# Start addresses of loaded tiles, the order of the last loads, and a permuted read of o, in a decode kernel that is bound by its loads

## Chip, cores and metric

One core of a Trainium2 chip; the other cores idle. The metric is the device time of one execution in microseconds (us), median of several. The kernel before takes 533.47 us (533.46 to 534.03, three runs).

## The reference, cut to what matters

```python
x  = A_x                                   # 4 x 1 x 640, bf16
xn = layernorm(x)
# A: attention of one new token, 32 heads of 192, over the last 2048 of 8192 cached keys
q  = xn @ wq                               # 640 -> 32*192
p  = softmax(q . k_cache[:, :, -2048:] * 192**-0.5)
oA = (p @ v_cache[:, :, -2048:]) @ wo      # 6144 -> 640
# B: gated feed-forward, 640 -> 1536 -> 640
oB = (silu(xn @ w1) * (xn @ w3)) @ w2
return x + oA + oB
```

K and V of the window are 32 heads x 4 sequences x 2048 x 192 x 2 B, twice: 201 MB of the 223 MB that are loaded. Each byte is used once, and the loads set the pace: their queue keeps the DMA engines busy for 98.6% of the span before.

## The kernel before, as far as the change touches it

```python
    const = ctx.enter_context(tc.tile_pool(name="const", bufs=1))      # x, masks, qbc, ...
    fpool = ctx.enter_context(tc.tile_pool(name="ffn", bufs=1))        # w1, w3, w2 in turn
    kpool = ctx.enter_context(tc.tile_pool(name="kt", bufs=KBUFS))     # 2 tiles of 24,576 B a partition
    vpool = ctx.enter_context(tc.tile_pool(name="vt", bufs=VBUFS))     # 3
    ppool = ctx.enter_context(tc.tile_pool(name="pr", bufs=PBUFS))
    wopool = ctx.enter_context(tc.tile_pool(name="wo", bufs=2))
    # ... cut
    def load_v(h):                         # load_k likewise
        vt = vpool.tile([P, NJ, Dh], BF16, tag="vt")
        nc.sync.dma_start(out=vt[:].rearrange("q j d -> q (j d)"),
                          in_=v_win[:, h].rearrange("b (p j) d -> p b (j d)", p=PB))
    # ... cut
    def ge_sum(h):                         # head sum: adds the four strips of o of one head
        for par in range(2):
            nc.tensor.matmul(po[sl, 0:Dh], lhsT=sel_w[:, par]..., rhs=o_sb[:, par * Dh:(par + 1) * Dh], ...)
    def ge_turn(hg):                       # divides by the softmax sums and turns o
        nc.vector.tensor_scalar_mul(out=og[:].rearrange("p i r -> p r i"),
                                    in0=po[:, 0:Dh].rearrange("p (r i) -> p r i", i=RPP), scalar1=...)
        nc.vector.transpose(out=oT..., in_=og...)
    # ... cut: the schedule is a list of slots; one slot is a quarter of a head
    # tail: K31 | V29, V30, V31, w2 first part, wo 7, w2 second, w2 third   (wo 6 ahead of K31)
```

A load of K or V goes to 128 partitions, one contiguous row of 24,576 B each. A head's path: multiply K by q on the vector engine (`mult`, tile pr), add on the tensor engine (`adder`, tile ps), softmax, weighted sum of V (`pv`, tile o_ps), head sum (tile po), and for every four heads a projection by wo into acc.

## Time and profile before

| | before |
|---|---|
| time, median | 533.47 us |
| span of the profiled run | 530.5 us |
| loaded | 222.97 MB |
| mean of a 24,576 B packet (slow ones over 1.2 of the median left out) | 916.4 ns |
| last load lands | 526.85 us |
| cast of the result starts | 527.44 us |

How to read it: a "packet" is one row of one load. The records of the kernel before hold 128 such packets for each load but those of x, and for each 16 packets of 4 B (the completion writes of the recorded texts, 9 ns each), and a load has 16 semaphore steps, one for each DMA engine. The records don't name the engine; but from one load's finish to the next an engine takes 7.315 us, eight rows of 914 ns, so I count 8 of the 128 rows of each load to an engine, 640 rows of data in the whole run. "Lands" is the last of the 16 steps, that is, the slowest engine: multiplies that wait for K start 0.02 us after it in the kernel before, and 1.85 to 4.78 us after the first step. Packet durations and semaphore steps are in the trace's records; no line of the page holds them.

### The profile page before, as it was taken

The numbers are of one execution on the slowest core, as the hardware profiler recorded it, in microseconds if no ns is written. First come the engines' busy times: TensorE is split into PE (matmuls) and PEld (weight loads), VectorE is DVE, ScalarE is ACT, GpSimd is POOL, SyncE is SP. The second block draws the span as 40 slices with busy tenths as digits, with TensorE's granted clock in tenths as the row PEclk, the third lists the DMA queues.
The fourth block names the chain that finished last, engine by engine and source line by source line (L and its number), as shares of the span: only waits on it lengthen the run. The fifth ranks groups of instructions, "written<-read, shape, count | busy, mean of one in ns | idle before, by whom it ended". The sixth has DMA issues, their size and how long they took to land.

```text
span 530.5 us, 5427 instructions
## 1 busy us (share of the span) xinstructions
PE 342.7 (65%) x2306; PEld 144.5 (27%) x2307; DVE 350.2 (66%) x435; ACT 45.6 (9%) x143; POOL 1.1 (0%) x8
## 2 busy tenths in 40 slices
PE   2765766674757586667558776576565775566774
PEld 1322322232312232223223232232222232222332
DVE  3179775775557667578646876676667776667941
ACT  2111100000201000000000000000000000000010
POOL 0000000000000000000000000000000000000000
PEclk9889988899858878789988897798997899889988
DMA  8999999999999999999999999999999999999995
GB/s 356 445 417 422 417 435 434 426 434 422 431 434 421 433 423 433 430 426 433 426 423 437 424 428 429 428 432 424 428 429 432 427 432 426 432 427 406 428 427 220
DMA packets 11575, 223.31 MB, mean 421 GB/s; under 512 B 1296, under 2 KB 1312, under 8 KB 2592
## 3 DMA queue, kind: packets, MB, share of 16 engines
q1 hardware_dynamic: 11536, 222.97, 98.6%
q8 instruction: 18, 0.29, 0.2%
q14 instruction: 5, 0.04, 0.0%
q10 hardware_dynamic: 16, 0.01, 0.0%
HBM read 222.96 MB, written 0.01 MB: 420 GB/s over the span
## 4 chain that ended last, share of the span: by engine, by line
DMA 60%; DVE 23%; PE 15%; ACT 1%; issue 1%; SPq 0%
DMA kt<-in_A_k_cache_dram 50%; DVE pr L215 15%; PE ps L226 8%; DMA w<-in_B_w_dram 6%; DVE sc L234 4%; DMA wt<-in_A_wq_dram 3%; PE qps L175 2%; PE po L303 2%; DVE og L308 1%; DVE z L270 1%; PE o_ps L278 1%; ACT ex L262 1%; PE acc L196 1%; DVE oT L311 1%; ACT L262 0%
## 5 line engine op out<-in xcount | busy, mean ns | idle before, releaser
L226 PE MATMUL ps<-pr,idb 128*128 128x512 bf16 x768 | 212.5, 418 | 161.8 <-DVE pr L215 161.8
L215 DVE TENSOR_TENSOR pr<-kt,qbc 128x3072 bf16<-128x3072 bf16 x128 | 223.3, 1745 | 110.6 <-DMA kt<-in_A_k_cache_dram 110.6
L226 PEld LDWEIGHTS <-idb 128*128 128x128 bf16 x768 | 76.2, 103 | 262.8 <-issue 206.4
L234 DVE TENSOR_REDUCE sc<-ps 128x16 f32<-128x512 f32 x128 | 87.0, 679 | 1.9 <-PE ps L226 1.9
L278 PE MATMUL o_ps<-vt,z 128*8 128x384 bf16 x1024 | 55.0, 353 | 5.5 <-DMA vt<-in_A_v_cache_dram 5.5
L303 PE MATMUL po<-o_sb,sel_w 128*32 128x192 f32 x128 | 35.0, 409 | 0.5 <-ACT o_sb L285 0.5
L278 PEld LDWEIGHTS <-z 128*8 128x8 bf16 x1024 | 25.1, 90 | 31.8 <-issue 20.4
L285 ACT COPY o_sb<-o_ps 128x384 f32<-128x384 f32 x32 | 15.3, 479 | 193.6 <-PE o_ps L278 193.6
L259 ACT COPY negm<-mt 128x1 f32<-128x1 f32 x32 | 5.1, 159 | 258.0 <-PE mt L256 258.0
L270 DVE TENSOR_TENSOR z<-ex,mask_b 128x256 bf16<-128x256 bf16 x32 | 13.4, 417 | 18.2 <-ACT ex L262 18.1
L175 PE MATMUL qps<-wt,xnT 128*128 128x512 bf16 x59 | 16.6, 443 | 5.1 <-DMA wt<-in_A_wq_dram 5.1
L303 PEld LDWEIGHTS po<-o_sb,sel_w 128*32 128x32 f32 x128 | 13.8, 130 | 20.9 <-issue 14.5
L181 DVE CAST qbc<-qps 128x512 bf16<-128x512 f32 x6 | 3.8, 685 | 18.5 <-PE qps L175 18.5
L308 DVE TENSOR_SCALAR og<-po,rt 128x192 bf16<-128x192 f32 x8 | 8.4, 1055 | 8.0 <-PE po L303 8.0
L248 DVE TENSOR_REDUCE gmax<-mt 1x4 f32<-1x128 f32 x32 | 8.8, 276 | 6.9 <-PE mt L243 6.8
L256 PEld LDWEIGHTS mt<-ones_ff,gneg 1*128 1x128 f32 x64 | 9.4, 182 | 13.4 <-issue 8.1
L256 PE MATMUL mt<-ones_ff,gneg 1*128 1x1 f32 x64 | 12.1, 256 | 0.0
L243 PE MATMUL mt<-idf,lmax 128*1 128x128 f32 x32 | 11.2, 351 | 1.1 <-DVE lmax L238 1.1
L196 PE MATMUL acc<-wo_t,oT 128*4 128x320 bf16 x96 | 10.3, 318 | 1.6 <-DVE oT L311 1.6
L262 ACT ACTIVATE ex<-sc,negm 128x64 bf16<-128x64 f32 x32 | 11.1, 348 | 1.0
L175 PEld LDWEIGHTS <-xnT 128*128 128x128 bf16 x60 | 6.6, 110 | 14.7 <-issue 9.1
L290 PEld LDWEIGHTS po<-rsum,tot_w 128*32 128x32 f32 x64 | 4.7, 112 | 14.7 <-issue 13.1
(52 smaller groups left out, 70.2 us busy)
## 6 DMA issues: line engine op xcount, KB each, us to landing
kt<-in_A_k_cache_dram SPq DMA_DIRECT2D x32, 3072.0 KB, 20.2
vt<-in_A_v_cache_dram SPq DMA_DIRECT2D x32, 3072.0 KB, 27.4
wo_t<-in_A_wo_dram SPq DMA_DIRECT2D x8, 960.0 KB, 21.0
wt<-in_A_wq_dram SPq DMA_DIRECT2D x2, 3072.0 KB, 9.8
w<-in_B_w_dram SPq DMA_DIRECT2D x2, 1920.0 KB, 25.0
wt<-in_A_wq_dram SPq DMA_DIRECT2D x1, 1536.0 KB
w<-in_B_w_dram SPq DMA_DIRECT2D x1, 1280.0 KB, 34.3
w<-in_B_w_dram SPq DMA_DIRECT2D x2, 320.0 KB, 36.4
```

The costliest lines, as they stand in the source:

```text
L175: nc.tensor.matmul(qp[:], lhsT=xnT[:, kc].rearrange("p a b -> p (a b)"), rhs=wq_rows[kc][:, (c0 + i) * QC:(c0 + i + 1) * QC], start=(kc == ...
L196: nc.tensor.matmul(acc[i * CT:i * CT + B, :], lhsT=lhsT, rhs=rhs[:, i * N0:(i + 1) * N0], start=first, stop=last)
L215: nc.vector.tensor_tensor(out=pr[:], in0=kts[h][:, g * JQ:(g + 1) * JQ, :], in1=qbc[:, h * Dh:(h + 1) * Dh].unsqueeze(1).to_broadcast([P, ...
L226: nc.tensor.matmul(ps[:], lhsT=idb[:], rhs=pr[:, :, kk * DD:(kk + 1) * DD], start=(kk == 0), stop=(kk == NK - 1))
L234: nc.vector.tensor_reduce(out=scs[h][:, g * JQ:(g + 1) * JQ], in_=pss.pop(u)[:], axis=AX.X, op=ALU.add)
L256: nc.tensor.matmul(mt[:, P:P + 1], lhsT=gneg[:].rearrange("o p b -> o (p b)"), rhs=ones_ff[0:1, 0:1], start=True, stop=True)
L262: nc.scalar.activation(out=ex[:], in_=scs.pop(h)[:], func=ACTF.Exp, bias=negm[:, 0:1], scale=SCALE, accum_out=rsum[:])
L270: nc.vector.tensor_tensor(out=z[:], in0=ex[:].unsqueeze(2).to_broadcast([P, NJ, B]), in1=mask_b[:].unsqueeze(1).to_broadcast([P, NJ, B]), ...
L278: nc.tensor.matmul(o_ps[c * CT:c * CT + 2 * B, :], lhsT=z[:, 2 * jj:2 * jj + 2, :], rhs=vt[:, 2 * jj:2 * jj + 2, :], start=(jj < 4), stop= ...
L285: nc.scalar.copy(out=o_sb[:], in_=o_ps[:])
L303: nc.tensor.matmul(po[sl, 0:Dh], lhsT=sel_w[:, par].rearrange("p a b -> p (a b)"), rhs=o_sb[:, par * Dh:(par + 1) * Dh], start=(par == 0), ...
L308: nc.vector.tensor_scalar_mul(out=og[:].rearrange("p i r -> p r i"), in0=po[:, 0:Dh].rearrange("p (r i) -> p r i", i=RPP), scalar1=rts.pop ...
```

## The change

The intent is threefold. The pools with loaded tiles go ahead of the constants, so that every loaded tile starts at a multiple of 256 B (before: 32 B past one). The last loads go in another order: V29 ahead of K31, V31 in halves, wo 6 behind the first part of w2. And o is permuted while the tensor engine reads it for the head sum, so that the vector engine writes it in order.

```diff
-    const = ctx.enter_context(tc.tile_pool(name="const", bufs=1))
+    head = ctx.enter_context(tc.tile_pool(name="head", bufs=1))
     fpool = ...; kpool = ...; vpool = ...
+    wopool = ctx.enter_context(tc.tile_pool(name="wo", bufs=2))
+    const = ctx.enter_context(tc.tile_pool(name="const", bufs=1))
     ppool = ...
-    wopool = ctx.enter_context(tc.tile_pool(name="wo", bufs=2))
 # ... cut: load_v(h, parts=1) loads in `parts` pieces along the row
-    tot_w = const.tile([P, NREP, B], FP32, name="tot_w")
+    tot_w = head.tile([P, NREP, B], FP32, name="tot_w")        # 128 B: brings the next pool to 256
 # ge_sum
-                             rhs=o_sb[:, par * Dh:(par + 1) * Dh], ...
+                             rhs=o_sb[:, par * Dh:(par + 1) * Dh].rearrange("p (r i) -> p i r", i=RPP), ...
 # ge_turn
-        nc.vector.tensor_scalar_mul(out=og[:].rearrange("p i r -> p r i"),
-                                    in0=po[:, 0:Dh].rearrange("p (r i) -> p r i", i=RPP), ...
+        nc.vector.tensor_scalar_mul(out=og[:].rearrange("p i r -> p (i r)"), in0=po[:, 0:Dh], ...
 # schedule
-        if h < H - 3:
+        if h < H - 2:
             add(u0 + 2, 0, load_v, h)
-    for h in range(H - 3, H):
-        add(NU - 6, 0, load_v, h)
+    for h in range(H - 2, H):
+        add(NU - 6, 0, load_v, h, 1 + (h == H - 1))
     add(NU - 6, 0, w2_load, 0)
+    add(NU - 6, 0, wo_load, NG - 2)
     add(NU - 6, 0, wo_load, NG - 1)
 # ... cut: pv of head 31 in halves, projection of wo 6 moved behind w2's first part
```

More of the change, by code (lines that the diff above doesn't have):

```diff
@@ L93, in load_k, with load_v @@
         kts[h] = kt
-    def load_v(h):
+    def load_v(h, parts=1):
         vt = vpool.tile([P, NJ, Dh], BF16, tag="vt")
-        nc.sync.dma_start(out=vt[:].rearrange("q j d -> q (j d)"),
-                          in_=v_win[:, h].rearrange("b (p j) d -> p b (j d)", p=PB))
+        src = v_win[:, h].rearrange("b (p j) d -> p b j d", p=PB)
+        n = NJ // parts
+        for j in range(0, NJ, n):
+            nc.sync.dma_start(out=vt[:, j:j + n, :].rearrange("q j d -> q (j d)"),
+                              in_=src[:, :, j:j + n, :].rearrange("p b j d -> p b (j d)"))
         vts[h] = vt
@@ L303, in ge_sum @@
             nc.tensor.matmul(po[sl, 0:Dh], lhsT=sel_w[:, par].rearrange("p a b -> p (a b)"),
-                             rhs=o_sb[:, par * Dh:(par + 1) * Dh], start=(par == 0), stop=(par == 1))
+                             rhs=o_sb[:, par * Dh:(par + 1) * Dh].rearrange("p (r i) -> p i r", i=RPP), start=(par == 0), stop=(par == 1))
     def ge_turn(hg):
         og = small.tile([P, RPP, CT], BF16, tag="og", bufs=1, name="og")
-        nc.vector.tensor_scalar_mul(out=og[:].rearrange("p i r -> p r i"),
-                                    in0=po[:, 0:Dh].rearrange("p (r i) -> p r i", i=RPP), scalar1=rts.pop(hg)[:, 0:1])
+        nc.vector.tensor_scalar_mul(out=og[:].rearrange("p i r -> p (i r)"), in0=po[:, 0:Dh],
+                                    scalar1=rts.pop(hg)[:, 0:1])
         oT = small.tile([P, RPP, CT], BF16, tag="oT", bufs=2, name="oT")
@@ L387 @@
         v, m = ends.get(h, (u0 + L, u0 + L + 1))
-        add(v, 7, pv, h)
+        if h < H - 1:
+            add(v, 7, pv, h)
+        else:
+            add(v - 1, 7, pv, h, 0, NJ // 2)
+            add(v, 7, pv, h, NJ // 2, NJ)
         add(m, 7, ge_sum, h)
@@ L407 @@
     add(17, 6, x_add, 1)
-    add((H - 3) * GQ + 1, 0, wo_load, NG - 2)
-    add(NU - 4, 6, ge_proj, NG - 2, 0, RPP // 2)
-    add(NU - 3, 6, ge_proj, NG - 2, RPP // 2, RPP)
-    for h in range(H - 3, H):
-        add(NU - 6, 0, load_v, h)
+    for h in range(H - 2, H):
+        add(NU - 6, 0, load_v, h, 1 + (h == H - 1))
     add(NU - 6, 0, w2_load, 0)
+    add(NU - 6, 0, wo_load, NG - 2)
     add(NU - 6, 0, wo_load, NG - 1)
@@ L418 @@
     add(NU - 6, 0, w2_load, 2)
-    add(e - 2, 8, ffn_out, 0)
+    add(e - 1, 8, ffn_out, 0)
+    add(e - 1, 8, ge_proj, NG - 2, 0, RPP)
     add(e, 6, ge_proj, NG - 1, 0, RPP)
```

## The prediction

Its windows are pieces of 256 B that start at multiples of 256 B: a row of 24,576 B touches 96 of them, and 97 where the tile starts 32 B past a multiple. That each costs the same 9.41 ns (913 ns in 97 parts) is my estimate from packet durations; no run had shown it.

> **What bounds the kernel now.** I read the page first: busy shares, the DMA row and the queues.
>
> ```profile
> span 530.5 us, 5427 instructions
> PE 342.7 (65%) x2306; PEld 144.5 (27%) x2307; DVE 350.2 (66%) x435; ACT 45.6 (9%) x143; POOL 1.1 (0%) x8
> DMA  8999999999999999999999999999999999999995
> q1 hardware_dynamic: 11536, 222.97, 98.6%
> ```
>
> No engine is over 66%; the queue of loads keeps the 16 DMA engines busy for 98.6% of the span. Next, the chain of work that ended last, half of it K loads:
>
> ```profile
> 83.94 1.77 DVE pr L215
> ...
> 113.18 1.76 DVE pr L215
> ...
> 444.28 1.76 DVE pr L215
> ...
> 473.53 1.77 DVE pr L215
> ```
>
> Each of these multiplies starts when its K lands. In both pairs four loads of 3072 KB pass, in 29.24 and 29.25 us: 7.31 us a load. A DMA engine carries 8 of the 128 rows of 24,576 B, so a row costs 914 ns. The trace's packet records agree: 8,448 packets of 24,576 B, one a row, median 915 ns.
>
> Third, do loads come late? The queue's waits, its issues, and the stretches of time:
>
> ```profile
> SPq L91 <- DVE pr L215: 323.9, 30, 13.0
> ...
> 41.02 0.54 SPq L91 DMA_DIRECT2D kt<-in_A_k_cache_dram  x1
> ...
> 485.09 0.53 SPq L91 DMA_DIRECT2D kt<-in_A_k_cache_dram  x1
> ```
>
> ```profile
> 42.00:44.00 2.00, 1.19 (x7) 0.43 (x6) 1.97 (x3) 0.00 (x0) 0.00 (x0) 1.00 0.87 307
> 60.00:480.00 420.00, 274.71 (x1866) 114.66 (x1865) 285.70 (x345) 31.59 (x108) 0.00 (x0) 0.88 1.00 429
> 485.00:487.00 2.00, 1.88 (x21) 0.79 (x24) 0.67 (x2) 0.00 (x0) 0.00 (x0) 1.00 0.90 324
> 525.00:527.00 2.00, 1.13 (x18) 0.80 (x20) 0.78 (x2) 0.00 (x0) 0.00 (x0) 1.00 0.17 64
> ```
>
> The last two columns are DMA share and GB/s. The issuing queue waits 324 us and it costs nothing: between 60 and 480 us the share is 1.00, because two more loads lie behind the one under way. The rings run dry twice, behind the issues at 41.02 and 485.09 us. At the end some engines finish early (share 0.17 in the last stretch). The semaphore records say how far apart the 16 engines are: the wo load before K31 finishes on its first engine at 485.71 and on its last at 490.48 us. From there to the last engine's finish of V30 at 512.42 us are 21.94 us, three loads of 7.31: the slowest engine never starved at 485 us. Only the quick ones did, and only the slowest sets the end. Its last piece of w2 lands at 526.85 us, and the timeline ends so:
>
> ```profile
> 525.87 0.98 PE L196 MATMUL acc<-wo_t,oT 128*4 128x320 bf16 x12 [1.57 <-DVE oT L311]
> 526.69 0.71 PE L196 MATMUL acc<-w,hT 128*4 128x320 bf16 x8
> 527.44 0.48 DVE L430 CAST res<-acc 36x320 bf16<-36x320 f32 x1 [1.62 <-PE acc L196]
> ```
>
> The result's cast starts 0.59 us after that landing; the last projection is ready at about the same time, so two paths end together.
>
> [...] In the built program of before every K, V, wq, wo and FFN tile starts 32 B past such a multiple[...]
>
> **The change, part by part.** (a) Alignment. The built program of after has all loaded tiles but the small x tiles at multiples of 256 B. My model, made from packet durations: each touched window of 256 B costs [...]9.41 ns, however few bytes are in it. It gives 97 x 9.41 = 913 ns for 24,576 B (trace 912 to 922), 31 x 9.41 = 292 for 7,680 B (trace 291 to 301, median 294), 49 x 9.41 = 461 for 12,288 B (trace 460), and one, 9.4, for the completion write of 4 B (trace 9). Aligned, each row sheds one. Rows: K and V 64 x 128 = 8,192, wq 384, wo 1,024, w1, w3 and w2 640: 10,240, or 640 an engine; 640 x 9.41 ns = 6.02 us. Not all of it reaches the end. The K issue at 41.02 us waits for multiplies behind the q projection, which follows only the wq loads. Those save 24 rows, 0.23 us; the next 24 rows (two K, one V) save another 0.23 us into an already dry ring. Left: 5.80 us. (b) V31 in halves: one more completion write an engine, 0.01 us lost. (c) V29 before K31, wo 6 at the end: the dry stretch at 485 us should go, but the slowest engine lost nothing there, so 0, though the sums of busy time will look better. (d) The tail: after V31 now come w2's first part, two wo and two small parts of w2: by the model 321 + 241 + 241 + 81 + 81 = 965 windows, 9.1 us, where before V31 landed 7.1 us ahead of the end. V31's second half needs its weighted sum (half of 2.73 us), copy 0.48, the head sum about 1.3, og, oT 0.38, projection 0.98: under 6 us, so it is now hidden. Alignment alone would have left this chain of some 7.6 us the later of the two, by about 0.3 us: the new order protects that and gains up to 0.1. (e) o permuted as the moving operand: eight og of 1.05 us become contiguous, about 0.3 us each (estimate from the qbc cast, 512 columns in 685 ns). 6 us of DVE, none on the path. The matmuls of the head sum (128 records, 35.0 us) read 4 B at a step of 24 B. If that doubles them PE gets 35 us more work and reaches 71% of the span: still no bound. Sum: 5.80 - 0.01 + 0.1, about 5.9 us; 533.47 - 5.9 = 527.6.
>
> **Rivals.** First, the 9 ns a packet are a fixed cost (turnaround) and not the extra window. For it: 4 B also take 9 ns, so an intercept of 9 ns fits all sizes. Against it: [...]the records have 9 and 29, which are one and three windows.[...] I give it one in eight. Second, the dry stretch at 485 us did cost the end, or the engines' lag comes out smaller: bytes missing in 485 to 490 us make about 0.75 us of all engines' time; the time would be 526.8. Third, the slow read of o becomes a wait: at the end, if the head sum took three times as long, V31's chain would pass the last w2 landing. The slack is some 3 us against 2.6 us more; unlikely, and then worth under 1 us: 528.5. Fourth, slow packets of about 1.4 us (23 between 60 and 480 us) make the slowest engine late; they may fall otherwise in the changed program, up to 1 us either way.
>
> **Range and chances.** The model explains the load rate to 0.1%, so most chance lies near 527.6, with the lag's 1 us either way and a tail for the first rival: 526.3 to 529.8 for 8 in 10. Faster by over 2% would be below 522.8 us[...]; 0.02. Slower by 2% needs a new bound: 0.01. Within 2%: 0.97.
>
> **What would show it.** Rows of 24,576 B at a median of about 905 ns in place of 915; four loads between K landings in 28.95 us (4 x 769 windows); GB/s of 433 to 434 in mid-kernel; no dry stretch near 480 us; the last w2 landing near 521 us, and the cast 0.5 to 0.6 us after it; og near 0.3 us; the head-sum matmuls dearer or not, with no change of the end. Wrong: rows still at 913 to 915 ns (first rival), or a cast that waits for the V31 chain.

## The result, and the profile after

The changed kernel takes 529.56 us (529.35 to 531.62, four runs) where the one before took 533.55 on the same occasion. The ratio is 0.9932, with a 95% interval of 0.9907 to 0.9957. Ratios here are the mean time of one kernel's fast runs over that of the other's of the same rounds, so not quite the ratio of the medians that I quote. A repeat on another chip gave 529.22 us and 0.9906 (0.9890 to 0.9923). So the gain is between 3.6 and 5.0 us; the forecast was 5.9. By the threshold of 2% the two are the same.

The page of the changed kernel, lines that answer to those of before:

```profile
span 527.6 us, 5428 instructions
PE 353.5 (67%) x2306; PEld 142.6 (27%) x2307; DVE 345.6 (65%) x435; ACT 45.6 (9%) x143; POOL 1.1 (0%) x8
DMA  8999999999999999999999999999999999999994
q1 hardware_dynamic: 11680, 222.97, 98.6%
```

The picture is the same: loads all the time, no engine near its limit. The chain of work that ended last:

```profile
411.38 1.76 DVE pr L219
...
440.47 1.77 DVE pr L219
...
469.56 1.76 DVE pr L219
```

Four loads now take 29.09 us in place of 29.25; I had forecast 28.95. Half of the step is there. The stretches of time (last two columns: DMA share and GB/s):

```profile
42.00:44.00 2.00, 1.19 (x6) 0.47 (x5) 1.97 (x3) 0.00 (x0) 0.00 (x0) 1.00 0.71 258
60.00:480.00 420.00, 283.87 (x1886) 113.91 (x1885) 287.68 (x352) 32.80 (x114) 0.00 (x0) 0.89 1.00 431
485.00:487.00 2.00, 1.06 (x3) 0.39 (x3) 1.97 (x4) 0.00 (x0) 0.00 (x0) 0.78 1.00 430
```

431 GB/s and not the forecast 433 to 434. The dry stretch at 485 us is gone, the one at 42 us is not. The packet records say what happened to a row (durations in ns, packets over 1.2 of the median left out):

```
packet of        24,576 B             7,680   10,240   12,288   15,360   2,560 B
before  mean     916.4                295.8   389.0    460.0    578.0    104.9
        most     915, 922, 912, 914   294     388      460      576      102
after   mean     912.2                291.0   385.0    460.0    573.0    102.0
        most     912 (99% 912 or 913) 291     385      460      573      102
```

Alignment took away the spread above the shortest duration and left the shortest where it was. Misaligned rows had been at 912 ns too: 303 of the 304 that start between 4 and 25 us in the kernel before are at 912 or 913 ns, the first rows of K among them. A load takes 7.275 us in place of 7.315, read from one finish of the first of the 16 engines to the next (81.89, 96.43, 110.99 us; before 82.06, 96.69, 111.32; two loads between each): 5.0 ns a row. (The row of 12,288 B is of wq, before the spread set in, and of V31's halves after.)

The end of the timeline, against 525.87, 526.69 and 527.44 us before:

```profile
523.05 0.98 PE L200 MATMUL acc<-wo_t,oT 128*4 128x320 bf16 x12 [0.40 <-DVE oT L315]
523.86 0.71 PE L200 MATMUL acc<-w,hT 128*4 128x320 bf16 x8
524.62 0.48 DVE L437 CAST res<-acc 36x320 bf16<-36x320 f32 x1 [1.62 <-PE acc L200]
```

The last load lands at 523.85 us, 3.00 us earlier; the cast starts 0.77 us after it (before 0.59). The projection still comes from oT and not from a landing: two paths still end together. And the groups of instructions for o (busy us and mean ns of one stand behind the first bar), on the page of before and then on the listing of after:

```profile
L303 PE MATMUL po<-o_sb,sel_w 128*32 128x192 f32 x128 | 35.0, 409 | 0.5 <-ACT o_sb L285 0.5
L308 DVE TENSOR_SCALAR og<-po,rt 128x192 bf16<-128x192 f32 x8 | 8.4, 1055 | 8.0 <-PE po L303 8.0
```

```profile
L307 PE MATMUL po<-o_sb,sel_w 128*32 128x192 f32 x128 | 49.1, 517 | 1.1 <-ACT o_sb L289 1.1
L312 DVE TENSOR_SCALAR og<-po,rt 128x192 bf16<-128x192 f32 x8 | 3.2, 404 | 3.7 <-PE po L307 3.6
```

og fell to 404 ns, the head sum's records rose from 409 to 517 ns mean; neither bounds anything.

### The profile page after: what moved, and what is told of

Its sections match the earlier page's. It is cut to its first block, busy times and chain, and to the rows that moved or that the text cites.

```text
span 527.6 us, 5428 instructions
## 1 busy us (share of the span) xinstructions
PE 353.5 (67%) x2306; PEld 142.6 (27%) x2307; DVE 345.6 (65%) x435; ACT 45.6 (9%) x143; POOL 1.1 (0%) x8
## 3 DMA queue, kind: packets, MB, share of 16 engines
q1 hardware_dynamic: 11680, 222.97, 98.6%
## 4 chain that ended last, share of the span: by engine, by line
DMA 57%; DVE 22%; PE 18%; ACT 2%; issue 1%; SPq 0%
DMA kt<-in_A_k_cache_dram 54%; DVE pr L219 15%; PE ps L230 9%; PE po L307 4%; DVE sc L238 3%; DMA wt<-in_A_wq_dram 3%; PE qps L179 2%; PE o_ps L282 2%; DVE z L274 1%; ACT ex L266 1%; PE mt L260 1%; DVE oT L315 1%; DVE og L312 0%; PE acc L200 0%; ACT L266 0%
## 5 line engine op out<-in xcount | busy, mean ns | idle before, releaser
L230 PE MATMUL ps<-pr,idb 128*128 128x512 bf16 x768 | 208.5, 412 | 152.3 <-DVE pr L219 152.3
L230 PEld LDWEIGHTS <-idb 128*128 128x128 bf16 x768 | 74.4, 102 | 258.7 <-issue 200.1
L282 PE MATMUL o_ps<-vt,z 128*8 128x384 bf16 x1024 | 60.6, 373 | 2.7 <-DMA vt<-in_A_v_cache_dram 2.7
L307 PE MATMUL po<-o_sb,sel_w 128*32 128x192 f32 x128 | 49.1, 517 | 1.1 <-ACT o_sb L289 1.1
L282 PEld LDWEIGHTS <-z 128*8 128x8 bf16 x1024 | 26.2, 94 | 32.8 <-issue 22.8
L200 PE MATMUL acc<-wo_t,oT 128*4 128x320 bf16 x96 | 9.2, 298 | 0.4 <-DVE oT L315 0.4
L242 DVE TENSOR_REDUCE lmax<-sc 128x1 f32<-128x64 f32 x32 | 7.0, 220 | 1.1
```

The lines of the kernel that those rows point to most:

```text
L200: nc.tensor.matmul(acc[i * CT:i * CT + B, :], lhsT=lhsT, rhs=rhs[:, i * N0:(i + 1) * N0], start=first, stop=last)
L230: nc.tensor.matmul(ps[:], lhsT=idb[:], rhs=pr[:, :, kk * DD:(kk + 1) * DD], start=(kk == 0), stop=(kk == NK - 1))
L282: nc.tensor.matmul(o_ps[c * CT:c * CT + 2 * B, :], lhsT=z[:, 2 * jj:2 * jj + 2, :], rhs=vt[:, 2 * jj:2 * jj + 2, :], start=(jj < 4), stop= ...
L307: nc.tensor.matmul(po[sl, 0:Dh], lhsT=sel_w[:, par].rearrange("p a b -> p (a b)"), rhs=o_sb[:, par * Dh:(par + 1) * Dh].rearrange("p (r i) ...
```

## The experiments

Theory A: alignment brings the gain, by taking the spread off the packets; about 8 ns a packet stay, as a fixed cost (7.8 ns by the aligned sizes, below). Rivals: the load order brings it; or the place of the constants. For the engines' lag, theory D: fetches of tensor instructions. "Last landing" and "lag" (first to last engine at that landing; the expectations call it the spread) are of the profiled run.

| run | time, us (range) | ratio to before (95%) | mean 24,576 B packet, ns | last landing, us | cast after it, us | lag, us |
|---|---|---|---|---|---|---|
| before | 533.47 (533.46-534.03) | 1 | 916.4 | 526.85 | 0.59 | 3.19 |
| the change | 529.56 (529.35-531.62) | 0.9932 (0.9907-0.9957) | 912.2 | 523.85 | 0.77 | 4.58 |
| align_only | 530.51 (529.31-531.20) | 0.9929 (0.9913-0.9944) | 912.2 | 523.61 | 1.81 | 4.10 |
| shift32 | 533.72 (532.34-534.92) | 0.9991 (0.9974-1.0008) | 916.4 | 528.52 | 0.52 | 6.16 |
| shift64 | 533.04 (532.02-534.40) | 0.9983 (0.9962-1.0003) | 915.5 | 528.52 | 0.52 | 4.87 |
| shift128 | 531.81 (531.80-531.89) | 0.9958 (0.9944-0.9972) | 915.3 | 526.42 | 0.52 | 4.97 |
| loads_shift32 | 525.73 (one look) | | 916.5 | 522.87 | | 1.07 |
| loads_aligned | 522.30 (one look) | | 912.0 | 519.43 | | 0.91 |
| halves | 533.83 (532.65-534.90) | 1.0005 (0.9985-1.0025) | two of 460.2 | 529.19 | 0.52 | 4.75 |
| v1_early | 529.02 (528.85-530.47) | 0.9927 (0.9915-0.9940) | 912.1 | 523.37 | 0.51 | 4.75 |
| k31_first | 530.09 (529.79-532.93) | 0.9944 (0.9926-0.9962) | | 526.74 | 1.23 | 3.05 |
| old_o | 529.78 (529.22-530.86) | 0.9931 (0.9915-0.9946) | | 524.67 | 1.07 | 4.58 |
| fewer_pe | 529.81 (529.25-531.50) | 0.9935 (0.9920-0.9951) | | 525.78 | 0.52 | 4.38 |
| combined | 529.66 (529.22-531.24) | 0.9929 (0.9914-0.9944) | | 524.46 | 0.52 | 3.65 |
| after_again | 529.22 (528.86-529.53) | 0.9906 (0.9890-0.9923) | | 523.57 | 0.95 | 4.26 |
| fewest_pe | 529.56 (529.15-530.25) | 0.9916 (0.9901-0.9932) | | 523.62 | 0.78 | 4.35 |
| fewest_v1 | 529.25 (528.76-529.64) | 0.9909 (0.9894-0.9923) | | 523.42 | 1.37 | 4.87 |
| no_max | 528.00 (527.46-528.60) | 0.9883 (0.9866-0.9900) | | 522.25 | 1.37 | 3.40 |

The profiled run of k31_first was the slowest of its six, those of old_o, fewer_pe and combined were among the slower of theirs; their landings are not compared with the others.

### Alignment alone, and taken away

align_only is the kernel before with the pools moved and tot_w in `head`; nothing else.

> The kernel before with the pools moved so that all loaded tiles start at multiples of 256 B, and nothing else of the change. Theory A (alignment takes the jitter out of the packets: 912 ns for nearly all rows of 24,576 B, mean 5 ns less than before; [...]the rest of the change gives nothing): the last landing about 3 us earlier than before, about 530 us, within 0.7 us of the whole change. Rival B (the gain comes from the new load order): packets as before, median 915 ns, and about 533.5 us.

The shifts put a pad of 32, 64 or 128 B ahead of tot_w in the changed kernel:

```diff
+    pad = head.tile([P, 8], FP32, name="pad")        # 16 for 64 B, 32 for 128 B
+    nc.vector.memset(pad[:], 0.0)
     tot_w = head.tile([P, NREP, B], FP32, name="tot_w")
```

> The changed kernel with a pad of 32 B ahead, so that every loaded tile is again 32 B past a multiple of 256 B; order of loads, o and halves as in the change. Theory A: packets of 24,576 B at 915 and 922 ns again, mean 917 to 918 ns, and about 533 us. Rival B: 912 ns and about 529.6 us, since the order is the changed one. Rival C (the place of the constants behind the tiles, not the alignment): as rival B.

> The changed kernel with every loaded tile 64 B past a multiple of 256 B. If what matters is the cut at 256 B: packets as with 32 B, 915 to 922 ns, about 533 us. If a multiple of 64 B is enough: 912 ns and about 529.6 us.

> The changed kernel with every loaded tile 128 B past a multiple of 256 B. If what matters is the cut at 256 B: packets at 915 to 922 ns, about 533 us. If a multiple of 64 or 128 B is enough: 912 ns and about 529.6 us.

Measured: alignment alone gives 0.9929, the whole change without alignment 0.9991. So alignment is the gain, and the rest of the change gives nothing that these runs can tell from zero (the intervals leave room for about 1 us). The constants' place is not it, since shift32 has that of the change. Neither 64 B nor 128 B is enough: the spread stays (means 915.5 and 915.3 ns), though shift128 has 43% of its rows at 912 or 913 ns against 13% of shift32, and its time is about half of the gain better (0.9958). What 128 B helps, and why, these runs don't show; nor do they show whether a row is cut at a multiple of 256 B. Only the end of the loads in SBUF was moved.

The end of align_only's timeline shows what the new tail is for:

```profile
523.86 0.98 PE L197 MATMUL acc<-wo_t,oT 128*4 128x320 bf16 x12 [1.57 <-DVE oT L312]
524.67 0.71 PE L197 MATMUL acc<-w,hT 128*4 128x320 bf16 x8
525.42 0.48 DVE L431 CAST res<-acc 36x320 bf16<-36x320 f32 x1 [1.62 <-PE acc L197]
```

Its last load had landed at 523.61 us; the cast now comes 1.8 us after it, behind the chain of V31. In the time it doesn't show against the whole change (0.9929 and 0.9932).

### Is the spread made by the engines' work?

Both kernels are the changed one with only the loads left after the q projection, misaligned and aligned. Their outputs are wrong, which doesn't matter for the times.

```diff
-            fn(*args)
+            if fn in (load_k, load_v, wo_load, ffn_load, w2_load, x_load):
+                fn(*args)
```

> Wrong result on purpose: the changed kernel with all tiles 32 B past a multiple of 256 B, and after the q projection only the loads, no multiplies, sums or projections. If the jitter comes from engines that read and write SBUF beside the loads: rows of 24,576 B at 912 ns throughout. If the misaligned start alone makes it, among the 16 DMA engines themselves: 915 and 922 ns as with the work.

> Wrong result on purpose: the same without the pad, tiles at multiples of 256 B. 912 ns rows under both readings; the floor for the loads, last landing near 521 us if the ring never runs dry.

Page and stretches of the misaligned one, then of the aligned one:

```profile
span 524.0 us, 320 instructions
q1 hardware_dynamic: 11680, 222.97, 99.6%
60.00:480.00 420.00, 0.00 (x0) 0.00 (x0) 0.00 (x0) 0.00 (x0) 0.00 (x0) 0.50 1.00 430
```

```profile
span 520.5 us, 319 instructions
q1 hardware_dynamic: 11680, 222.97, 99.7%
60.00:480.00 420.00, 0.00 (x0) 0.00 (x0) 0.00 (x0) 0.00 (x0) 0.00 (x0) 0.50 1.00 432
```

No engine works between 60 and 480 us, and the misaligned rows are at 915 and 922 ns all the same (mean 916.5); the aligned ones are at 912 (99.7% at 912 or 913). So the spread comes from the misaligned loads themselves and not from work beside them. The price of the misalignment is read here almost alone, from one look at each: 522.87 - 519.43 = 3.44 us at the last landing. What delays a misaligned row is not shown; that the misaligned rows of the first 25 us in the kernel before escape it (303 of 304 at 912 or 913 ns), and 26 of the 37 that start there between 44 and 46 us, just behind the dry ring (DMA share 0.87 from 42 to 44 us), says only that it isn't a fixed cost of each.

### The 8 ns that stay

halves cuts every K and V row in two. Aligned, as the change. The text has two readings of the 8 ns that aligned packets still carry: a fixed cost of a packet (theory A: half rows of 460 ns, about 534 us), or an extra window of the model (452 ns, about 530 us).

```diff
-        nc.sync.dma_start(out=kt[:].rearrange("q j d -> q (j d)"), in_=...)
+        for j in range(0, NJ, NJ // 2):
+            nc.sync.dma_start(out=kt[:, j:j + NJ // 2, :].rearrange("q j d -> q (j d)"), in_=src[:, :, j:j + NJ // 2, :]...)
-    def load_v(h, parts=1):
+    def load_v(h, parts=2):
```

> The changed kernel (aligned) with every K and V load cut in two along the row, so that 504 more packets of 12,288 B a DMA engine are needed for the same bytes (63 loads; V31 is in halves already). [...]packets of 460 ns, two for 920 in place of 912, and 504 x about 8 ns = 4 us more, plus 63 completion writes of 9 ns = 0.6 us: about 534 us. If they are an extra window: aligned halves touch 48 windows each, packets of 452 ns and no loss beyond 0.6 us: about 530 us.

The number of packets, in the DMA lines of the page of halves and of the change:

```profile
DMA packets 20792, 223.32 MB, mean 419 GB/s; under 512 B 2320, under 2 KB 2336, under 8 KB 3616
```

```profile
DMA packets 11719, 223.31 MB, mean 423 GB/s; under 512 B 1312, under 2 KB 1328, under 8 KB 2608
```

A half row takes 460.2 ns, so two take 920.4 where one whole row takes 912.2: 8.2 ns a packet, though 12,288 B at a multiple of 256 B touch exactly half the windows. 504 x 8.2 ns + 63 x 9 ns = 4.7 us; the time rose from 529.56 to 533.83 us, 4.3 (3.9 by the ratios). The 8 ns are a fixed cost of a packet. The aligned means of the table above agree: from 2,560 to 24,576 B they grow by 36.8 ns per 1,000 B, which leaves 7.8 ns at 2,560 B and puts 7,680 B at 290.4 ns (measured 291.0). This is what the first rival of the prediction says.

### The tail and o

```diff
 # k31_first: V29 again behind K31 (h < H - 3, range(H - 3, H)), all else as changed
 # old_o: ge_sum and ge_turn as before the change, all else as changed
```

> The changed kernel with K31 loaded ahead of V29, as before the change; aligned, V31 in halves, w2 and wo 6 as changed. Theory A (the tail of the change waits for head 31's softmax, whose K lands one load later than it could, and ends 0.2 us behind the last landing): the cast of the result 0.5 to 0.6 us after the last landing in place of 0.77, the dry stretch of the quick engines near 480 us back, the last landing unchanged: 0.2 us less, about 529.3 us. Rival (the new place of V29 saved time of the slowest engine): 0.5 us or more slower.

> The changed kernel with o as before: read in order by the matmuls of the head sum, and turned by the vector engine. Head-sum records back from 517 to about 350 ns, og back from 0.40 to 1.05 us. In the tail four head-sum records give back about 0.7 us and og takes 0.65: no change, 529.5 us within 0.3. Rival (the slow read of o costs time elsewhere): 0.5 us or more faster.

k31_first came out at 530.09 us and 0.9944, which is no gain and perhaps a small loss; its interval overlaps that of the change, so the 0.2 us that I looked for are neither shown nor excluded. Its one trace is of its slowest run (532.93 us), with the tensor engine's granted clock at 0.50 from 526 to 528 us, and can't settle it. old_o is 529.78 us, 0.9931: no difference, as expected. Its groups:

```profile
L307 PE MATMUL po<-o_sb,sel_w 128*32 128x192 f32 x128 | 34.5, 404 | 1.1 <-ACT o_sb L289 1.1
L312 DVE TENSOR_SCALAR og<-po,rt 128x192 bf16<-128x192 f32 x8 | 8.4, 1053 | 2.8 <-PE po L307 2.8
```

The permuted read costs the tensor engine 14.6 us in all, and the vector engine is spared 5.2; at the end about 0.65 us of og are traded for four dearer records.

### The dry ring at 42 us

v1_early issues V1's load ahead of K2's, whose issue waits until 41 us.

```diff
-            add(u0 + 2, 0, load_v, h)
+            add(2 if h == 1 else u0 + 2, 0, load_v, h)
```

> The changed kernel with the load of V1 issued ahead of that of K2, so that a load lies in the rings while K2's issue waits for the multiplies of head 0 at 41 us. Theory A (the slowest engine loses about 1.9 us there: 9.2 us from V0's to K2's last landing where a load takes 7.28): no dry stretch at 42 us, last landing 1.5 to 1.9 us earlier, but the tail's chain of engine work (0.2 us behind the landing already) gives some back: about 528.0 us. Rival (only the quick engines starve, as at 485 us before): no change, 529.6 us.

```profile
42.00:44.00 2.00, 1.46 (x6) 0.58 (x6) 2.00 (x3) 0.00 (x0) 0.00 (x0) 1.00 0.92 393
```

The share rose from 0.71 to 0.92, but the time only fell to 529.02 us (0.9927), within the noise of the change. V1's slowest engine still finished 8.33 us behind V0's, where 7.27 is a load: another microsecond was lost, at about 49 us by the records, with a full ring. That led to theory D.

### What makes the slowest engine late

The page lists 18 packets of 16 KB on a queue for instructions. The records have them every 28 us or so from 49 us on, and the lag, the gap between first and last engine, grows in jumps. In the changed kernel they come with the load that lands at 53 (+1.55 us), 276 (+1.44) and 515 us (+1.43); fetches 1, 9 and 17 start at 48.9, 271.3 and 505.5 us. At the end seven engines (the first among them) stand within 0.8 us, eight are 2.5 to 3.3 us behind, one is 4.58: none, two and three jumps' worth. The fetches' durations repeat after eight (first, ninth and seventeenth 967, 961 and 961 ns, third and eleventh 884 and 880). So the fetches seem to go round eight of the engines, and the one with three is last. (The last fetch comes too late to count, which leaves seven engines with two; the eighth may owe its lag to the packets of 8 KB on q14, a second queue for instructions. The records don't name the engine.)

The packet records also show how a jump is made. In the change 17 of the 18 fetches, 0.88 to 0.97 us long, end within 0.02 us of the start of a row that takes 0.45 to 0.55 us longer than others of its size. Fetch and delay together are 1.40 to 1.44 us each time, which is the size of the jumps. All 19 slow rows of the change between 60 and 480 us stand behind a fetch or behind one of four packets of 8 KB on q14. And the two kernels with loads only, which have no fetch of 16 KB, end with a lag of 1.07 and 0.91 us.

The tensor engine has 4,613 records, 256 to each of 18 fetches. Three kernels take tensor instructions away to test it, and two join this with other edits:

```diff
 # fewer_pe: one record for two in these matmuls (po: 64 in place of 128)
-    o_sb, sel_w, gneg in FP32; rhs=ones_ff[0:1, 0:1]
+    o_sb, sel_w, gneg in BF16; rhs=idb[0:1, 0:1]
 # fewest_pe: rsum copied to BF16 too, with a BF16 copy of tot_w; fewest_v1: that with v1_early's edit
 # no_max: fewest_pe without lmax, its transpose, gmax and broadcast; exp with a bias of 0
 # combined: fewer_pe + v1_early + k31_first
```

> The changed kernel with the head sum's operands and the broadcast of the maximum in bf16, so that each of these matmuls is one pass and not two: 96 matmuls and as many weight loads fewer on the tensor engine (of 4,613 records). Theory D (the slowest DMA engine is late by the fetches of 16 KB of tensor instructions, one engine in turn about every 28 us; the one that carried the 1st, 9th and 17th is last, and the 17th then falls near or after the end of the loads): spread between first and last engine at the last landing 3.1 to 3.3 us in place of 4.6, last landing up to 1.4 us earlier, 528.2 to 528.8 us. Rival (the lag comes from elsewhere): spread 4.6 us, 529.5 us.

> Alignment and the tail of the change, with V1 ahead of K2, K31 ahead of V29 and the matmuls in bf16. If the three add: V1 0.5 us, K31 0.2 us, fewer fetches up to 1.4 us: about 527.4 us. If the fetches don't matter: about 528.8 us.

> fewer_pe with the sum of the softmax denominators in bf16 too: 32 more matmuls and weight loads fewer, 4,357 tensor records. Theory D: the 17th fetch near 524 us, behind the last rows; two jumps of the lag in place of three, spread at the last landing 2.7 to 3.2 us, last landing 1.2 to 1.4 us earlier than its twin, about 1.2 us faster. Rival: three jumps, no change.

> The changed kernel once more as the twin of the other two on one chip: ratio 0.993, jumps near 50, 277 and 515 us.

> fewest_pe with V1 loaded ahead of K2. Theory D and the dry ring at 42 us together: 0.5 us below fewest_pe, 1.7 us below the changed kernel. Rival: as v1_early, 0.5 us below the changed kernel.

> fewest_pe without the maximum of the softmax (its scores are small in this data, so the result stays right; an experiment, not a kernel to keep): about 128 more tensor records fewer, 4,229, so 16 fetches. Theory D: jumps of the lag near 52 and 300 us and no third, spread at the last landing 2.8 to 3.2 us, last landing about 522.2 us, time about 528.2 us (1.0 to 1.4 us below the changed kernel). Rival: a third jump near 515 to 523 us all the same, 529.3 us.

| run | fetches | the 9th and 17th start at, us | jumps of the lag, at the landing of, us |
|---|---|---|---|
| after_again | 18 | 272.0, 505.2 | 52, 276, 514 (and 0.34 at 221) |
| fewer_pe | 17 | 283.3, 519.0 | 54, 300, 522 |
| fewest_pe | 17 | 289.3, 518.5 | 52, 297, 522 |
| fewest_v1 | 17 | 288.2, 518.0 | 52, 297, 522 |
| no_max | 16 | 295.1, none | 52, 84, 297, 329 |

The pages of fewer_pe, fewest_pe and no_max have 4,421, 4,358 and 4,230 tensor records, for 17, 17 and 16 fetches.

fewer_pe, combined, fewest_pe and fewest_v1 gained nothing: a 17th fetch came earlier than I had reckoned, still inside the loads, and the third jump came with it. That is a miss of my sizing, and it tells for the cause: the jumps moved with the fetches, from 276 to 297-300 and from 514 to 522 us. no_max has 16 fetches, no jump after 329 us, and lands its last load at 522.25 us. The instruction queue on its page, and on that of the change:

```profile
q8 instruction: 16, 0.26, 0.2%
```

```profile
q8 instruction: 18, 0.29, 0.2%
```

It ran in 528.00 us, 0.9883, against 0.9906 of after_again: 1.2 us. (They ran on different chips; the ratios are each to the kernel before on the same chip, and the intervals overlap by 0.001, so this gain of time is not clear of noise. Its cast came 1.37 us after the landing: the granted clock was 0.50 from 520 to 526 us, and the last eight matmuls took 1.28 us where the change's took 0.71.) What the traces show is the jump and its absence. no_max also has 94 vector records less, but the vector engine waits for K anyhow: its multiplies sat idle 147.4 us for it there and 111.3 us in after_again. It is correct for this data only because the scores are small; it is no kernel to keep. So no kept version beats the change beyond the noise.

## Why the prediction was wrong, point by point

- **The bound** (loads, slowest engine): right. The share stayed at 98.6%, and in loads_aligned the same bytes landed at 519.43 us.
- **Term (a), the alignment: this step failed.** It said that an aligned row sheds a whole window of 9.41 ns, 640 x 9.41 = 6.02 us. The fit from which it came (97, 31, 49 and 1 windows) could not tell 96 windows and a fixed cost from 97 windows, as the first rival said; I took packets of 80 B and 640 B (9 and 29 ns) as the judge, and they misled: by the rival, at 7.8 ns and 36.8 ns per 1,000 B, one of 640 B takes 31 ns, and the four of the result's write in the kernel before are at 29, 29, 31 and 35. Measured: 5.0 ns a row in the step from load to load, 640 x 5.0 = 3.2 us; 3.44 us in the pair with loads only. The 8 ns stay (halves: 8.2 ns a packet). What alignment takes away is a spread of 4 to 5 ns on average (4.2 by the means of 916.4 and 912.2, 5.0 by the step), which neither side of my argument had. I had the line in hand: misaligned rows of exactly 912 ns stood in the first 25 us of the kernel before, beside 915 and 922 later, and I fitted the lowest and called the rest scatter.
- **The loss at the first dry ring**, put at 0.23 us: of the right sign, but too small. Up to K2's landing the profiled run was 0.30 us later than before (52.56 against 52.26 us), where with 5.0 ns a row for 48 rows it should have been up to 0.24 us earlier; 471.29 us followed in place of 474.59, 3.30 us less, of which 592 rows x 5.0 ns make 2.96.
- **Term (c)**: that the dry stretch at 485 us cost the slowest engine nothing was right as far as runs tell: with the new order the share there is 1.00, and shift32, which has this order and no alignment, is no faster than before (0.9991). The sums did look better, as forecast: the first engine finished 4.39 us earlier than before, the last 3.00.
- **Term (d), the tail**: the chain behind V31 was put at under 6 us and hidden. It took 9.98 us in the profiled run, from V31's landing at 514.64 to the cast at 524.62, because head 31's softmax was only ready at 515.0, K31 being loaded behind V29, and V30's sum stood before V31's on the tensor engine at 2.73 us. The cast came 0.77 us after the landing, 0.2 us later than forecast. That alignment alone would leave the old tail late was right in kind, 1.81 us in place of some 0.9.
- **Term (e), o**: right in that it sets nothing. The head sum's records rose by a quarter, not to double; PE is at 67%. og came to 0.40 us where 0.3 was forecast.
- **The fourth rival**, the lag of the slowest engine, was left as 1 us either way. It is 3.0 to 4.9 us in the profiled runs of the aligned kernels with whole rows and full work (4.58 in the change). Its slow packets are the rows behind the fetches of instructions (17 of 24,576 B over 1.2 of the median between 60 and 480 us in the kernel before, not 23), and one jump of the lag was removed with its fetch.

Together: forecast 5.9, of which (a) lost 2.8 and the tail 0.2 to 0.3; that leaves 2.9 us, which is what the profiled spans show (530.5 to 527.6). The ratios show 3.6 us (0.9932) to 5.0 (after_again). That 529.56 us still lies between 526.3 and 529.8 is owed to the room left there for the lag and the first rival, not to the working.

What stays open: how misaligned loads are delayed, what the fixed 8 ns are, why the fetches go to so few engines, and whether K31 ahead of V29 would help by a few tenths.

## What to carry to other kernels

Where loads fill the time, look at the durations of single packets: a floor shared by all and a spread above it are two costs with two cures. Starting loaded tiles at multiples of 256 B removed the spread here (starts 32, 64 and 128 B past one did not); longer rows are what thins the fixed 8 ns (two halves took 920.4 ns, a whole row 912.2); a fit over sizes alone can't tell which one alignment will remove, so test it with one pad. Of the 16 engines the last was 4.58 us behind the first at the end of the change, and the end belongs to the slowest: ask what that one carries beside the data.
